# Pinned order, deeper prefetch and two moved constants on the GpSimd load queue of a linear-attention and spectral-mixing kernel

## The chip, the cores and the metric

One core of one Trainium2 chip. The metric is the device time of one execution in microseconds (us), the median of several runs; the trace is that of one of these runs. The program uses one core only, with the kernel before run beside each changed kernel on the same chip.

## The reference, cut to what matters

```python
# q, k, v: (8 batches, 8 heads, 576, 64) fp32
phi = lambda x: where(x > 0, x, exp(x) - 1) + 1
kv  = einsum('bhsd,bhse->bhde', phi(k), v);  z = sum(phi(k), axis=2)
x   = einsum('bhsd,bhde->bhse', phi(q), kv) / (einsum('bhsd,bhd->bhs', phi(q), z)[..., None] + 1e-6)
# x -> (8, 576, 512); 64 modes, each with complex weights of 512 x 512
X = rfft(x, axis=1)
Y[:, :64] = einsum('bmd,mde->bme', X[:, :64], w_r + 1j * w_i)
u = x + irfft(Y, n=576, axis=1)
out = u + maximum(u @ w_ch, 0)
```

The 128 weight matrices are most of the bytes. As bf16 on the chip each is 512 KB; one batch of q, of k or of v as fp16 is 576 KB.

## The kernel before

All large loads go through GpSimd's queue, because they change the type on the way (fp32 to fp16 or bf16). The attention stage makes the spectrum `xt_c`, batch by batch. Modes start only when the last batch's spectrum is there. Until then, weights can only be prefetched, into 8 buffers that stay and `W_PRE` buffers that are freed after the early modes. The framework's scheduler may reorder the instructions of an engine unless told otherwise.

```python
    nc.sync.dma_start(out=pick_sb, in_=pick_dr.ap())     # small constants, on SyncE's queue
    nc.sync.dma_start(out=inv_sb, in_=inv_dr.ap())
    # ... cut ...
    W_KEEP = 8
    def w_load(kk, half, pool, tag, bufs):
        name, src = (("wr", moe_w_r), ("wi", moe_w_i))[half]
        w = pool.tile([128, NDC, D], BF16, tag=tag, bufs=bufs, name=f"{name}{kk}")
        nc.gpsimd.dma_start(out=w, in_=src[kk].rearrange("(p dc) e -> p dc e", dc=NDC))
        return w
    W_PRE = 10
    # ... cut ...
    for b in range(B):                                    # attention, one batch at a time
        raw = {}
        for nm, src in (("q", q), ("k", k), ("v", v)):    # two buffers each
            t = sA.tile([128, NHP, NJ * Dh], F16, tag=f"{nm}16", bufs=2, name=f"{nm}16_{b}")
            nc.gpsimd.dma_start(out=t, in_=src[b].rearrange("h s d -> (h s) d").rearrange(
                "(hp r j) d -> r hp (j d)", r=128, j=NJ))
            raw[nm] = t
        if b >= 1:
            w_next()                                      # one prefetched weight per batch
        for nm in ("q", "k"):                             # ACT: exp; DVE: max, then min
            # ... cut ...
            for c in range(2):
                nc.vector.tensor_tensor(out=ev[:, c], in0=ev[:, c], in1=rv[:, c], op=ALU.min)
        nc.vector.tensor_copy(out=vp[:, :, :, 0:64], in_=raw["v"]...)   # the copy of v
        # ... cut: kv, numerators, spectrum of the batch into xt_c ...

    nc.gpsimd.dma_start(out=wch16, in_=moe_w_ch.rearrange("(c p) j -> p c j", p=128))
    while pending:
        w_next()                                          # the rest of the prefetch
    # ... cut: 64 modes, each with two weights; inverse transform ...
    def finish(t, by_act):                                # output stage
        # ... cut ...
        if by_act:
            nc.scalar.activation(out=r, in_=e, func=AF.Relu)
            nc.gpsimd.tensor_tensor(out=x, in0=x, in1=r, op=ALU.add)
```

The last use of the k buffer of batch b is the `min` of k, and DVE does it just after the copy of v of batch b+1 (its own order, shown below). The k load of batch b+2 needs that buffer. The constant `pick_sb` is an operand of a matmul in every mode, `inv_sb` one of the inverse transform.

Of the kernel before, what the change touches and what calls it, by code (L numbers as in the profile page):

```python
# [16 lines left out]
NJ = 9  # L17
# [36 lines left out]
def kernel(  # L54
# [10 lines left out]
    nc = tc.nc  # L65
# [5 lines left out]
    NDC = D // 128  # L71
# [9 lines left out]
    inv_dr = nc.inline_tensor(inv_np, name="dft_inv")  # L81
    pick_dr = nc.inline_tensor(pick_np, name="row_pick")
# [7 lines left out]
    inv_sb = const.tile([2 * NM, S], F16, name="inv_sb")  # L90
    pick_sb = const.tile([128, 16], F16, name="pick_sb")
    wch16 = const.tile([128, NDC, D], F16, name="wch16")
# [2 lines left out]
    nc.scalar.activation(out=actwarm, in_=actwarm, func=AF.Exp)  # L95
    nc.sync.dma_start(out=id16, in_=id16_dr.ap())
    nc.sync.dma_start(out=fwd_sb, in_=fwd_dr.ap())
    nc.sync.dma_start(out=pick_sb, in_=pick_dr.ap())
    nc.sync.dma_start(out=inv_sb, in_=inv_dr.ap())

    xt_c = xpool.tile([128, XTW], BF16, name="xt_c")
    nc.vector.memset(xt_c[:, NDC * XDC : XTW], 0.0)
# [15 lines left out]
    def w_load(kk: int, half: int, pool, tag: str, bufs: int):  # L118
        name, src = (("wr", moe_w_r), ("wi", moe_w_i))[half]
        w = pool.tile([128, NDC, D], BF16, tag=tag, bufs=bufs, name=f"{name}{kk}")  # L120
        nc.gpsimd.dma_start(out=w, in_=src[kk].rearrange("(p dc) e -> p dc e", dc=NDC))  # L121
        return w

    w_in: dict[int, list] = {}


    W_PRE = 10
    wpre_ctx, sA_ctx, psA_ctx = ExitStack(), ExitStack(), ExitStack()
    wpre = wpre_ctx.enter_context(tc.tile_pool(name="wpre", bufs=1))
    sA = sA_ctx.enter_context(tc.tile_pool(name="sA", bufs=1))  # L130
    psA = psA_ctx.enter_context(tc.tile_pool(name="psA", bufs=1, space=bass.MemoryType.PSUM))
    n_pre, n_keep = W_PRE // 2, W_KEEP // 2

# [6 lines left out]
    def w_next():  # L140
        kk, half = pending.pop(0)
        pool, tag, bufs = (wpool, "w", W_KEEP) if kk < n_keep else (wpre, "wp", W_PRE)
        w_in.setdefault(kk, []).append(w_load(kk, half, pool, tag, bufs))
# [17 lines left out]
    for b in range(B):  # L161
        raw = {}
        for nm, src in (("q", q), ("k", k), ("v", v)):
            t = sA.tile([128, NHP, NJ * Dh], F16, tag=f"{nm}16", bufs=2, name=f"{nm}16_{b}")
            nc.gpsimd.dma_start(
                out=t,
                in_=src[b].rearrange("h s d -> (h s) d").rearrange(
                    "(hp r j) d -> r hp (j d)", r=128, j=NJ
                ),
            )  # L170
            raw[nm] = t
        if b >= 1:
# [3 lines left out]
        for nm in ("q", "k"):  # L176

            e = sA.tile([128, 2, NJ, 2, Dh], F16, tag=f"{nm}e", bufs=2, name=f"{nm}e_{b}")
# [3 lines left out]
            for c in range(2):  # L182
                nc.scalar.activation(out=ev[:, c], in_=rv[:, c], func=AF.Exp)  # L183
            nc.vector.tensor_scalar(  # L184
                out=rf, in0=rf, scalar1=0.0, scalar2=1.0, op0=ALU.max, op1=ALU.add
# [6 lines left out]
            out=vp[:, :, :, 0:64], in_=raw["v"].rearrange("p a (j d) -> p a j d", d=Dh)  # L192
# [17 lines left out]
        for hpo in range(2):  # L210
            rows = slice(hpo * 64, hpo * 64 + 64)
            nc.scalar.copy(
                out=kv_sb[rows],
                in_=kv_ps[rows, :, 0:260].rearrange("p t (c o n) -> p c t o n", c=2, o=2)[
                    :, :, :, hpo, :
                ],
# [5 lines left out]
        for hpp in range(2):  # L222
            qT_ps = psA.tile([128, NJ, 2, NP], F16, tag="big", bufs=3, name=f"qTp{b}_{hpp}")
            for sl in range(NJ):
                j = 8 if sl == 8 else 4 * (sl % 2) + sl // 2
# [6 lines left out]
                out=qT[:, hpp].rearrange("p t (j r) -> p t j r", r=NP),  # L232
                in_=qT_ps.rearrange("p j t r -> p t j r"),
# [5 lines left out]
        for jj in range(NJJ + 1):  # L239
# [8 lines left out]
                out=dst.rearrange("p (o c d) -> p o c d", o=2, c=4),  # L248
# [19 lines left out]
    def w_get(kk: int):  # L268
        if kk not in w_in:
            w_in[kk] = [w_load(kk, half, wpool, "w", W_KEEP) for half in range(2)]  # L270
        return w_in.pop(kk)
# [24 lines left out]
                yt_ps[:, ec, kk % 8, :], st[:, ec * 128 : ec * 128 + 128], pick_sb  # L296
            )

    nc.gpsimd.dma_start(out=wch16, in_=moe_w_ch.rearrange("(c p) j -> p c j", p=128))
    while pending:  # L300
        w_next()
    psA_ctx.close()
    sA_ctx.close()
    psW = tc.alloc_tile_pool(name="psW", bufs=1, space=bass.MemoryType.PSUM)
# [170 lines left out]
    for b in range(B):  # L475
        ov = out[b].rearrange("(p j) d -> p j d", j=NJ)
        for jj in range(NJJ):
            finish(b * NJJ + jj, jj % 2 == 1)
            if jj % 2 == 1:
                for j2 in range(2):  # L480
                    (nc.sync, nc.scalar)[j2].dma_start(
                        out=ov[:, 4 * j2 + jj - 1 : 4 * j2 + jj + 1, :],
                        in_=x_main[b][j2 * 64 : j2 * 64 + 64, jj - 1 : jj + 1, :],
                    )
        if b % 2 == 1:
            i = b // 2
            finish(B * NJJ + i, False)
            for hf in range(2):
                (nc.sync, nc.scalar)[hf].dma_start(
                    out=out[2 * i + hf].rearrange("(p j) d -> p j d", j=NJ)[:, 8, :],  # L490
                    in_=x_tail[i][hf * 64 : hf * 64 + 64, :],
# [32 lines left out]
```

## Time and profile before

| Kernel before | |
|---|---|
| median time (range) | 454.02 us (453.87 to 454.76) |
| profiled span | 452.8 us |
| loads issued by GpSimd | 153, 81.80 MB landed |
| last spectrum copy | 123.84 us |
| matmul on the last weight | 400.38 us |

The page first. It names the engines PE (TensorE; PEld is its loading of operands), DVE (VectorE), ACT (ScalarE), POOL (GpSimd) and SP (SyncE); a q behind a name marks the engine's sequencer. The DMA row gives the busy share of the DMA engines in tenths, in 40 slices of the span (11.3 us each); the next row gives the bytes that landed per second in each slice. The last line is the chain of waits, by engine.

```profile
DMA  9999999999689999999999999999999999925884
GB/s 156 211 209 209 208 207 210 210 213 214 126 164 213 214 214 213 212 214 214 214 214 214 212 214 214 214 214 213 214 212 214 214 213 214 213 48 173 271 263 147
DMA 64%; PE 15%; DVE 11%; ACT 4%; issue 2%; POOL 1%; POOLq 0%; DVEq 0%; ACTq 0%; SPq 0%
```

The kernel is bound by its loads up to slice 35. 214 GB/s landed are 428 GB/s read, since the type is halved on the way. The Trainium skill ("DMA: Bandwidth & Descriptors", Bandwidth) has 425 GB/s for a 16 MB transfer on this path, so the queue runs at its rate here. The one gap is in slices 11 and 12 (126 and 164 GB/s). In stretches of 2 us, the view by windows shows it. Its columns are the stretch, its length, the busy time (and number of instructions) of PE, PEld, DVE, ACT and POOL, the granted clock, the DMA share and GB/s.

```profile
58.00:60.00 2.00, 0.72 (x13) 0.48 (x15) 2.00 (x8) 2.00 (x4) 1.09 (x2) 0.64 1.21 207
60.00:62.00 2.00, 1.81 (x24) 1.14 (x24) 2.00 (x6) 1.16 (x2) 0.94 (x2) 0.50 1.20 207
...
118.00:120.00 2.00, 1.31 (x12) 0.64 (x11) 1.93 (x7) 0.00 (x0) 0.00 (x0) 0.50 0.90 182
120.00:122.00 2.00, 1.53 (x10) 0.92 (x10) 0.41 (x1) 0.00 (x0) 0.00 (x0) 0.50 0.16 31
122.00:124.00 2.00, 1.08 (x7) 0.57 (x6) 0.69 (x1) 0.15 (x1) 0.00 (x0) 0.50 0.00 0
124.00:126.00 2.00, 1.72 (x16) 0.80 (x20) 0.49 (x1) 0.23 (x1) 0.53 (x1) 0.50 0.00 0
126.00:128.00 2.00, 2.00 (x21) 0.69 (x13) 0.26 (x2) 0.58 (x1) 1.59 (x3) 0.50 0.67 90
```

Missing bytes in the last five, against 214 GB/s: (32 + 183 + 214 + 214 + 124) x 2 / 214 = 7.2 us. That is the hole that the change aims at. At 58 to 62 us, inside attention, nothing is missing. GpSimd's timeline says why there is a hole (start, length, what was issued, and in brackets the idle time before it and what ended it):

```profile
46.36 0.74 POOL L165 DMA_DIRECT2D v_5_924<-in_v_dram  x1 [5.52 <-DVE rd_87 L245]
52.69 0.74 POOL L165 DMA_DIRECT2D q_5_920<-in_q_dram  x1 [5.58 <-issue]
...
58.91 0.74 POOL L165 DMA_DIRECT2D k_5_922<-in_k_dram  x1 [4.94 <-issue]
...
80.46 0.74 POOL L165 DMA_DIRECT2D k_7_1248<-in_k_dram  x1 [2.42 <-DVE ke_934 L188]
...
102.32 0.53 POOL L121 DMA_DIRECT2D wi_1430<-in_moe_w_i_dram  x1 [1.93 <-DMA wi_1414<-in_moe_w_i_dram]
125.27 0.53 POOL L121 DMA_DIRECT2D wr_1603<-in_moe_w_r_dram  x1 [22.42 <-PE P_1442 L279]
```

The last prefetched weight was issued at 102.32 us. The next load waited 22.42 us for mode 0's matmuls to free a buffer. The first lines show the scheduler's order: v_5 is issued 6.3 us ahead of q_5 and 12.6 us ahead of k_5, against the program's q, k, v. So v_5 had long landed when DVE came to it, and DVE went on to the min of k_4 without a wait:

```profile
66.94 0.75 DVE L191 COPY vpad_104<-v_5_924 128x2304 f16<-128x2304 f16 x1
67.61 1.42 DVE L188 TENSOR_TENSOR ke_771<-ke_771,k_4_759 128x1152 f16<-128x1152 f16 x2
```

On ACT, the last batch waited for q and for k, and its spectrum was done at 123.84 us:

```profile
94.33 2.22 ACT L183 ACTIVATE qe_1254<-q_7_1246 128x1152 f16<-128x1152 f16 x2 [3.25 <-DMA q_7_1246<-in_q_dram]
99.60 2.22 ACT L183 ACTIVATE ke_1260<-k_7_1248 128x1152 f16<-128x1152 f16 x2 [3.06 <-DMA k_7_1248<-in_k_dram]
...
123.84 0.38 ACT L265 ACTIVATE xt_c<-xf_1386 128x256 bf16<-128x256 f32 x1 [7.76 <-DVE xt_c L264]
```

First the matmul on the last weight in PE's timeline, then the last instructions of the program by line (count, then shortest, median and longest in ns, then the first and last start in us):

```profile
400.38 0.67 PE L285 MATMUL P_3689<-wi_3687,xt_c 128*32 128x512 bf16 x4 [1.82 <-DMA wi_3687<-in_moe_w_i_dram]
```

### The profile page before, as it was taken

To read this page: it belongs to the slowest core of one execution; us is meant where nothing else is said; L and a number is where in the kernel's file an instruction comes from. 1 tells how busy PE (TensorE), PEld (TensorE's weight loads), DVE (VectorE), ACT (ScalarE), POOL (GpSimd) and SP (SyncE) were. 2 spreads that over 40 slices of the span, in tenths; PEclk is the share of its full clock that TensorE was granted. 3 is DMA by queue.
4 is the path that set the end of the run, shared out by engine and by line. 5 is a ranking of instruction groups with operands and counts; after the bars stand their busy time and mean duration, and the time that the engine had idled before them with its cause. 6 is when DMAs were issued, how large, how long until landed. Compare 5 with 4: busy or idle time off the path is not lost.

```text
span 452.8 us, 6147 instructions
## 1 busy us (share of the span) xinstructions
PE 270.5 (60%) x2488; PEld 147.4 (33%) x2488; DVE 181.2 (40%) x329; ACT 136.8 (30%) x207; POOL 107.9 (24%) x173
## 2 busy tenths in 40 slices
PE   0353777767699777766777643233332399359870
PEld 0332555545434334333334321111110168113320
DVE  0672788865424353434344400100100022019990
ACT  3566256642224343343343411000000023013120
POOL 4222124210033222222212212122212221004650
PEclk9955556656556999999899975555555569559995
DMA  9999999999689999999999999999999999925884
GB/s 156 211 209 209 208 207 210 210 213 214 126 164 213 214 214 213 212 214 214 214 214 214 212 214 214 214 214 213 214 212 214 214 213 214 213 48 173 271 263 147
DMA packets 35691, 92.23 MB, mean 204 GB/s; under 512 B 3536, under 2 KB 16592, under 8 KB 35664
## 3 DMA queue, kind: packets, MB, share of 16 engines
q0 software_dynamic: 31632, 81.80, 93.1%
q1 hardware_dynamic: 2304, 5.20, 3.9%
q10 hardware_dynamic: 1728, 4.85, 3.4%
q8 instruction: 19, 0.31, 0.2%
q14 instruction: 8, 0.07, 0.0%
HBM read 163.93 MB, written 9.44 MB: 383 GB/s over the span
## 4 chain that ended last, share of the span: by engine, by line
DMA 64%; PE 15%; DVE 11%; ACT 4%; issue 2%; POOL 1%; POOLq 0%; DVEq 0%; ACTq 0%; SPq 0%
DMA wr_3038<-in_moe_w_r_dram 4%; DMA wi_2350<-in_moe_w_i_dram 4%; DMA k_7_1248<-in_k_dram 4%; DMA wi_2161<-in_moe_w_i_dram 4%; DMA wi_2009<-in_moe_w_i_dram 4%; DMA wr_2697<-in_moe_w_r_dram 4%; DMA wr_2861<-in_moe_w_r_dram 4%; DMA wr_3378<-in_moe_w_r_dram 4%; DMA wr_2546<-in_moe_w_r_dram 4%; DMA wr_3202<-in_moe_w_r_dram 4%; DMA wr_3480<-in_moe_w_r_dram 4%; DMA wi_1856<-in_moe_w_i_dram 4%; DMA wi_3687<-in_moe_w_i_dram 4%; DMA v_4_761<-in_v_dram 4%; DMA q_2_431<-in_q_dram 3%; DMA v_0_111<-in_v_dram 2%
## 5 line engine op out<-in xcount | busy, mean ns | idle before, releaser
L285 PEld LDWEIGHTS <-xt_c 128*32 128x32 bf16 x256 | 18.2, 156 | 70.5 <-issue 68.8
L279 PEld LDWEIGHTS <-xt_c 128*32 128x32 bf16 x256 | 15.4, 156 | 39.2 <-issue 21.8
L202 PE MATMUL kvp_126<-vpad_103,ke_119 64*128 64x130 f16 x36 | 2.1, 309 | 17.0 <-DVE ke_119 L188 17.0
L394 PEld LDWEIGHTS <-YT 128*112 128x112 f16 x32 | 7.7, 289 | 2.7 <-issue 2.2
L469 POOL TENSOR_TENSOR x_main_1583<-x_main_1583,r_3743 128x512 f32<-128x512 f32 x1 | 1.3, 1270 | 26.9 <-DVE x_main_1583 L465 26.9
L398 PEld LDWEIGHTS <-YT 128*112 128x112 f16 x32 | 7.5, 293 | 0.4
L202 PEld LDWEIGHTS <-ke_119 64*128 64x128 f16 x36 | 1.9, 141 | 17.0 <-DVE ke_119 L188 17.0
L152 PEld LDWEIGHTS <-qT_328 64*128 64x128 f16 (+1 forms) x80 | 2.6, 111 | 12.1 <-DVE x_1_351 L247 8.2
L121 POOL DMA_DIRECT2D wr_1603<-in_moe_w_r_dram x1 | 0.5, 531 | 22.4 <-PE P_1442 L279 22.4
L448 PEld LDWEIGHTS <-inv_sb 128*128 128x128 f16 x32 | 3.1, 97 | 7.3 <-issue 5.2
L444 PEld LDWEIGHTS <-id_64 128*128 128x128 f16 x32 | 3.1, 101 | 6.4 <-issue 2.4
L152 PE MATMUL num_3_386<-kv_79,qT_328 64*128 64x65 f16 x8 | 0.4, 239 | 7.9 <-DVE x_1_351 L247 7.9
L152 PEld LDWEIGHTS <-qT_165 64*128 64x128 f16 (+1 forms) x80 | 2.4, 120 | 7.5 <-ACT qT_165 L231 4.4
L291 DVE CAST ys_2962<-P_2953 128x512 f16<-128x512 f32 x1 | 0.7, 692 | 10.1 <-PE P_2953 L285 10.1
L184 DVE TENSOR_SCALAR q_0_107<-q_0_107 128x2304 f16<-128x2304 f16 x1 | 0.8, 760 | 9.7 <-ACT qe_113 L183 9.7
L152 PEld LDWEIGHTS <-qT_980 64*128 64x128 f16 (+1 forms) x80 | 2.5, 101 | 6.5 <-issue 3.4
L447 PEld LDWEIGHTS <-inv_sb 128*128 128x128 f16 x32 | 3.1, 97 | 4.4 <-issue 1.3
L291 DVE CAST ys_3679<-P_3670 128x512 f16<-128x512 f32 x1 | 0.7, 690 | 9.3 <-PE P_3670 L285 9.3
L291 DVE CAST ys_3391<-P_3382 128x512 f16<-128x512 f32 x1 | 0.7, 691 | 9.2 <-PE P_3382 L285 9.2
L291 DVE CAST ys_2809<-P_2800 128x512 f16<-128x512 f32 x1 | 0.7, 692 | 9.2 <-PE P_2800 L285 9.2
L291 DVE CAST ys_3051<-P_3042 128x512 f16<-128x512 f32 x1 | 0.7, 692 | 9.2 <-PE P_3042 L285 9.2
L291 DVE CAST ys_3429<-P_3420 128x512 f16<-128x512 f32 x1 | 0.7, 692 | 9.1 <-PE P_3420 L285 9.1
(1357 smaller groups left out, 857.6 us busy)
## 6 DMA issues: line engine op xcount, KB each, us to landing
q_0_107<-in_q_dram POOLq DMA_DIRECT2D x1, 576.0 KB, 7.8
k_0_109<-in_k_dram POOLq DMA_DIRECT2D x1, 576.0 KB, 9.7
v_0_111<-in_v_dram POOLq DMA_DIRECT2D x1, 576.0 KB, 11.8
q_1_268<-in_q_dram POOLq DMA_DIRECT2D x1, 576.0 KB, 13.9
k_1_270<-in_k_dram POOLq DMA_DIRECT2D x1, 576.0 KB, 16.0
v_1_272<-in_v_dram POOLq DMA_DIRECT2D x1, 576.0 KB, 18.1
q_2_431<-in_q_dram POOLq DMA_DIRECT2D x1, 576.0 KB, 14.5
k_2_433<-in_k_dram POOLq DMA_DIRECT2D x1, 576.0 KB, 13.3
```

Source lines behind the costliest of these rows:

```text
L152: nc.tensor.matmul(num[orow, hpo, c0 : c0 + 65], qT[rows, hpp, h2, cols], kv_sb[rows, hpp, h2, :])
L184: nc.vector.tensor_scalar(out=rf, in0=rf, scalar1=0.0, scalar2=1.0, op0=ALU.max, op1=ALU.add)
L202: nc.tensor.matmul(kv_ps[:, h2, hpp * 130 : hpp * 130 + 130], kp[rows, hpp, j].rearrange("p o d -> p (o d)"), vp[rows, hpp::2, j, 0:65], s ...
L279: nc.tensor.matmul(P[quad, :], xt_cols(dc, 1, kk), wr[:, dc, :], start=True, stop=False, tile_position=(0, dc * 32),)
L285: nc.tensor.matmul(P[quad, :], xt_cols(dc, 0, kk), wi[:, dc, :], start=False, stop=True, tile_position=(0, dc * 32),)
L291: nc.vector.tensor_copy(out=st, in_=P)
L394: nc.tensor.matmul(z_ps[: 2 * NE, :], lhs[ec], wch16[:, ec, :], start=(ec == 0), stop=(ec == NDC - 1))
L398: nc.tensor.transpose(y_ps[: 2 * NE, ec, :], lhs[ec], id16)
L444: nc.tensor.matmul(e, id16, e0_parts(t)[0][1], start=True, stop=False, skip_group_check=True)
L447: nc.tensor.matmul(y, lhs, YZ[b][:, 0, :])
L448: nc.tensor.matmul(e, lhs, YZ[b][:, 1, :], start=False, stop=True, skip_group_check=True)
L469: nc.gpsimd.tensor_tensor(out=x, in0=x, in1=r, op=ALU.add)
```

## The change

The intent: every load of the attention stage in program order, so that q and k of the last batches aren't overtaken; two more prefetched weights (ten modes) and two constants at the end of the prefetch, to fill the hole. The diff, with a wrapped load cut:

```diff
-    nc.sync.dma_start(out=pick_sb, in_=pick_dr.ap())
-    nc.sync.dma_start(out=inv_sb, in_=inv_dr.ap())
@@ w_load
-        nc.gpsimd.dma_start(out=w, in_=src[kk].rearrange("(p dc) e -> p dc e", dc=NDC))
+        tc.keep_in_program_order(
+            nc.gpsimd.dma_start(out=w, in_=src[kk].rearrange("(p dc) e -> p dc e", dc=NDC))
+        )
-    W_PRE = 10
+    W_PRE = 12
@@ loads of q, k and v
-            nc.gpsimd.dma_start( ... )
+            tc.keep_in_program_order(nc.gpsimd.dma_start( ... ))
@@ after attention
-    nc.gpsimd.dma_start(out=wch16, in_=moe_w_ch.rearrange("(c p) j -> p c j", p=128))
     while pending:
         w_next()
+    tc.keep_in_program_order(
+        nc.gpsimd.dma_start(out=wch16, in_=moe_w_ch.rearrange("(c p) j -> p c j", p=128))
+    )
+    tc.keep_in_program_order(nc.gpsimd.dma_start(out=pick_sb, in_=pick_dr.ap()))
+    tc.keep_in_program_order(nc.gpsimd.dma_start(out=inv_sb, in_=inv_dr.ap()))
```

More of the change, by code (lines that the diff above doesn't have):

```diff
@@ L164 @@
             t = sA.tile([128, NHP, NJ * Dh], F16, tag=f"{nm}16", bufs=2, name=f"{nm}16_{b}")
-            nc.gpsimd.dma_start(
-                out=t,
-                in_=src[b].rearrange("h s d -> (h s) d").rearrange(
-                    "(hp r j) d -> r hp (j d)", r=128, j=NJ
-                ),
+            tc.keep_in_program_order(
+                nc.gpsimd.dma_start(
+                    out=t,
+                    in_=src[b].rearrange("h s d -> (h s) d").rearrange(
+                        "(hp r j) d -> r hp (j d)", r=128, j=NJ
+                    ),
+                )
             )
@@ L297, in mode_product @@
             )
-    nc.gpsimd.dma_start(out=wch16, in_=moe_w_ch.rearrange("(c p) j -> p c j", p=128))
     while pending:
         w_next()
+    tc.keep_in_program_order(
+        nc.gpsimd.dma_start(out=wch16, in_=moe_w_ch.rearrange("(c p) j -> p c j", p=128))
+    )
+    tc.keep_in_program_order(nc.gpsimd.dma_start(out=pick_sb, in_=pick_dr.ap()))
+    tc.keep_in_program_order(nc.gpsimd.dma_start(out=inv_sb, in_=inv_dr.ap()))
     psA_ctx.close()
```

## The prediction

"Drain moves from 120.3" is the time at which the load queue runs empty.

> **What bounds the kernel now.** The page shows the DMA engines at 90% or more in nearly every slice up to 390 us: 214 GB/s in the mode stage, 206 to 212 while q, k and v stream. The chain of waits is 64% DMA; from 145 us it is one weight load after another until the last lands at 400.4 us. 52 us follow without loads (inverse transform, output), which the change leaves alone. So time = loaded bytes / rate + idle time of the load queue + 52 us, and only the idle time can be won.
>
> The DMA rates of stretches of 2 us show one large hole: 182, 31, 0, 0, 90 GB/s from 118 to 128 us, against 214 GB/s about 7.2 us. GpSimd's timeline says why: the last prefetched weight was issued at 102.3 us, and the next issue (125.3 us) needs mode 0's products to free a buffer. Mode 0 starts at 124.3 us, after the last batch's spectrum is copied.
>
> **What the change does.**
> 1. Two more prefetched weights, 512 KB each, 2.45 us each at 214 GB/s: 4.9 us more work before the hole.
> 2. pick and inv (148 KB, about 0.7 us) go from the start to the end of the prefetch: another 0.7 us in the hole.
> 3. Program order: the comparison of instruction orders shows that in the attention stage only GpSimd's order changes. Before, other loads went ahead of q_7 and k_7; k_7 landed at 99.6 us and ACT stood 3.1 us for it (3.3 us for q_7), with copies of older batches behind it. In program order k_7 should land near 87 us, v_7 near 90 us. So attention should end about 2 us sooner, near 122 us.
>
> **Cost side.** v_5 to v_7 can't overtake q and k any more. DVE needs v of batch b+1 before it finishes k of batch b, which frees the buffer for k of batch b+2. That loop: copy 0.7 + minimum 1.4 + issue 0.5 + 1.9 until data flows (wr_1603, issued at 125.3 us into an empty queue, shows bytes from about 127.1) + k and v 2.8 each + landing 0.5 = 10.6 us, against 3 x 2.83 + 2.45 = 10.9 us of DMA and about 11.0 us of computing per batch. The queue stays just fed; I allow 0 to 2 us of bubbles, an estimate. The Trainium skill ("DMA: Bandwidth & Descriptors", the anatomy of a SWDGE DMA) gives about 2.0 us of fixed cost per DMA; here wr_1603 took 5.0 us less 2.45 of data, 2.5 us.
>
> pick now lands last, near 127 us, so mode 0's gather matmul waits and PE stalls 2 to 4 us after about 2.5 modes. Their buffers are free by then (five loads, 12 us of queue), so this should not reach the queue. One more early mode (1.3 us of PE) is covered: the queue had 10 us of slack at 136 us.
>
> **Sum.** Drain moves from 120.3 to about 126 us, new loads are issued from about 123 us: the hole closes. 454.0 - 7.2 + 0.7 (bubbles) = 447.5 us, 1.4% faster. Range 445.8 to 450.5. Faster by over 2% would need 9 us, more than the idle there is. Chances: 0.05 faster, 0.94 within 2%, 0.01 slower.
>
> **What would show it.** No slice between 105 and 140 us below 200 GB/s; last weight landing near 393 us; 52 us behind it; ACT's waits for q_7 and k_7 gone; last spectrum copy near 122 us; a PE wait for pick.
>
> **What would make it wrong.** Head-of-line bubbles in attention (below 200 GB/s at 60 to 95 us); attention ending after 124 us; the pick wait holding back the releases of modes 2 and on; a changed rate of mixed loads.

## More of the kernel before

```profile
L519 POOLq DRAIN  x3: 45/102/11355, 440.4 to 452.5; - x3
L519 SPq DRAIN  x3: 7/7/7, 448.4 to 452.0; - x3
```

At its end GpSimd has a `DRAIN`, an instruction that the kernel's code does not ask for (the profile puts it to the framework's line `with TileContext`), of 11.36 us, from 440.38 to 451.73 us in the trace. Its last add ends at 442.41 us, so 9.3 us of the `DRAIN` lie behind all of GpSimd's work that the program asks for. SyncE has confirmed the last stores at 448.47 us. The program ends only after both, so it stands 451.73 - 448.47 = 3.26 us for GpSimd alone.

## The result

| | before | after |
|---|---|---|
| median time (range) | 454.02 us (453.87 to 454.76) | 450.03 us (448.93 to 450.39) |
| ratio to before | | 0.9905, 95% interval 0.9885 to 0.9925 |
| last spectrum copy | 123.84 us | 127.15 us |
| matmul on the last weight | 400.38 us | 399.83 us |
| stores confirmed (SyncE) | 448.47 us | 447.46 us |
| GpSimd's DRAIN | 440.38 to 451.73 us | 439.77 to 442.80 us |
| profiled span | 452.8 us | 448.5 us |

A ratio is the mean time of one kernel's fast runs over that of the other's of the same rounds, so not quite the ratio of the medians. By the time alone the prediction holds: 450.03 us lies inside 445.8 to 450.5, near its edge. By the trace the last weight, which should have come 7 us earlier, came 0.55 us earlier. The profile after, the same views:

```profile
DMA  8999999999999999999999999999999999953897
GB/s 139 209 210 209 208 177 179 178 214 213 214 192 216 212 215 213 214 213 214 213 214 214 213 214 213 214 213 213 214 213 214 213 214 213 214 104 92 275 284 217
```

Slices 11 and 12 have 214 and 192 GB/s now. But slices 6 to 8 fell from about 209 to about 178 GB/s, and the first slice from 156 to 139. By windows:

```profile
58.00:60.00 2.00, 0.34 (x9) 0.25 (x9) 2.00 (x6) 2.00 (x3) 0.70 (x1) 0.50 1.07 184
60.00:62.00 2.00, 1.81 (x25) 1.10 (x21) 2.00 (x7) 1.54 (x2) 1.32 (x3) 0.50 0.70 77
62.00:64.00 2.00, 2.00 (x29) 1.66 (x28) 2.00 (x4) 0.00 (x0) 0.00 (x0) 0.50 1.16 196
...
72.00:74.00 2.00, 1.26 (x19) 0.77 (x19) 2.00 (x6) 1.28 (x2) 1.81 (x3) 0.50 0.73 94
74.00:76.00 2.00, 2.00 (x29) 1.57 (x31) 1.91 (x4) 0.00 (x0) 0.21 (x1) 0.50 0.99 157
...
84.00:86.00 2.00, 0.84 (x17) 0.60 (x17) 2.00 (x8) 2.00 (x3) 1.20 (x2) 0.50 0.91 154
86.00:88.00 2.00, 1.81 (x26) 1.13 (x22) 2.00 (x5) 0.76 (x1) 2.00 (x4) 0.50 0.84 92
...
130.00:132.00 2.00, 0.39 (x1) 0.10 (x1) 0.00 (x0) 0.23 (x1) 2.00 (x5) 0.50 0.74 110
```

The first seven lines lack (23 + 130 + 11 + 113 + 50 + 53 + 115) x 2 / 207 = 4.8 us of loading: three new bubbles, one per batch. The last line is what is left of the hole, (214 - 110) x 2 / 214 = 1.0 us. GpSimd's timeline and DVE's copies of v show what the bubbles wait for:

```profile
59.30 0.74 POOL L166 DMA_DIRECT2D k_5_920<-in_k_dram  x1 [5.49 <-issue]
...
72.19 0.74 POOL L166 DMA_DIRECT2D k_6_1083<-in_k_dram  x1 [6.61 <-ACT qe_926 L185]
72.92 0.75 POOL L166 DMA_DIRECT2D v_6_1085<-in_v_dram  x1
...
84.80 0.74 POOL L166 DMA_DIRECT2D k_7_1246<-in_k_dram  x1 [5.77 <-ACT qe_1089 L185]
...
129.63 0.54 POOL L120 DMA_DIRECT2D wr_1622<-in_moe_w_r_dram  x1 [11.63 <-PE P_1461 L287]
```

```profile
69.56 0.76 DVE L193 COPY vpad_102<-v_5_922 128x2304 f16<-128x2304 f16 x1 [2.45 <-PE num_2_699 L152]
70.23 1.42 DVE L190 TENSOR_TENSOR ke_769<-ke_769,k_4_757 128x1152 f16<-128x1152 f16 x2
...
82.17 0.76 DVE L193 COPY vpad_101<-v_6_1085 128x2304 f16<-128x2304 f16 x1 [1.81 <-DMA v_6_1085<-in_v_dram]
```

This is a closed loop. v_5 lands at 69.4 us (the page's list of issues: 9.4 us after its issue at 60.03). DVE copies it at 69.56 us and then ends the min of k_4 at 71.65 us. That frees the buffer, and k_6 is issued at 72.19 us. v_6 stands behind k_6 in program order and lands at 82.1 us (9.2 us after 72.92). DVE copies it at 82.17 us, and so on. One turn takes 12.6 us. (In before, v_5 had been issued at 46.36 us, landed at 62.1 and was copied at 66.94 without a wait.) The label "ACT qe_926" in the bracket of k_6 is only what ended last by the profile's reckoning before that issue; the buffer is freed by DVE. In the same way the copy of v_5 names PE, though v_5 had landed only about 0.1 us before.

The attention stage therefore ends later, the pick constant makes PE wait 1.88 us, and the last weight comes 0.55 us earlier:

```profile
127.15 0.38 ACT L267 ACTIVATE xt_c<-xf_1384 128x256 bf16<-128x256 f32 x1 [7.75 <-DVE xt_c L266]
```

```profile
132.27 0.25 PE L297 MATMUL yt_1445<-pick_sb,ys_1455 128*128 128x16 f16 x4 [1.88 <-DMA pick_sb<-row_pick]
...
399.83 0.67 PE L287 MATMUL P_3689<-wi_3687,xt_c 128*32 128x512 bf16 x4 [1.77 <-DMA wi_3687<-in_moe_w_i_dram]
```

```profile
L525 POOLq DRAIN  x3: 46/102/3027, 439.8 to 448.0; - x3
L525 SPq DRAIN  x3: 7/7/7, 447.4 to 447.7; - x3
```

GpSimd's DRAIN takes 3.03 us in place of 11.36, ends 1.0 us after its last add and before the stores do. The span's 4.3 us are: 0.55 from the last weight, 0.46 between it and the confirmed stores, and 3.26 because nobody waits for GpSimd any more.

How closely do two traces agree? d2 below is after with two idle instructions more, and its last weight is used at 398.24 us, 1.6 us earlier than in after. The timed runs of after alone span 448.93 to 450.39 us, and its trace is of the slowest of them. So a difference of less than about 1.6 us between single traces of the pinned kernels is not resolved. The unpinned ones agree better: 400.38 to 400.58 us in before, d1, f2 and f3.

So there are two questions. Where did 7 us of filled hole go? And what makes the DRAIN short?

### The profile page after: what moved, and what is told of

Its sections match the earlier page's. It is cut to its first block, busy times and chain, and to the rows that moved or that the text cites. A ratio compares the mean times of both kernels' runs of the same rounds, so it can differ in the third digit from the quotient of the medians.

```text
span 448.5 us, 6143 instructions
## 1 busy us (share of the span) xinstructions
PE 272.3 (61%) x2488; PEld 150.6 (34%) x2488; DVE 180.7 (40%) x329; ACT 136.8 (31%) x207; POOL 109.7 (24%) x175
## 4 chain that ended last, share of the span: by engine, by line
DMA 70%; PE 10%; DVE 8%; issue 4%; ACT 3%; POOL 2%; POOLq 0%; ACTq 0%; DVEq 0%; SPq 0%
DMA wr_3038<-in_moe_w_r_dram 4%; DMA wi_1423<-in_moe_w_i_dram 4%; DMA wr_3378<-in_moe_w_r_dram 4%; DMA wr_2367<-in_moe_w_r_dram 4%; DMA wi_1820<-in_moe_w_i_dram 4%; DMA wr_2205<-in_moe_w_r_dram 4%; DMA wr_2697<-in_moe_w_r_dram 4%; DMA wr_2861<-in_moe_w_r_dram 4%; DMA wr_2520<-in_moe_w_r_dram 4%; DMA wr_3202<-in_moe_w_r_dram 4%; DMA wi_3687<-in_moe_w_i_dram 4%; DMA wr_3480<-in_moe_w_r_dram 4%; DMA wr_2026<-in_moe_w_r_dram 4%; DMA v_4_759<-in_v_dram 4%; DMA q_2_429<-in_q_dram 3%
## 5 line engine op out<-in xcount | busy, mean ns | idle before, releaser
L152 PEld LDWEIGHTS <-qT_326 64*128 64x128 f16 (+1 forms) x80 | 2.8, 115 | 13.5 <-DVE x_1_349 L249 8.8
L152 PEld LDWEIGHTS <-qT_163 64*128 64x128 f16 (+1 forms) x80 | 2.7, 112 | 8.2 <-ACT qT_163 L233 4.4
L152 PEld LDWEIGHTS <-qT_652 64*128 64x128 f16 (+1 forms) x80 | 2.5, 107 | 8.7 <-DVE x_3_675 L249 3.3
L152 PEld LDWEIGHTS <-qT_978 64*128 64x128 f16 (+1 forms) x80 | 2.5, 112 | 6.4 <-DVE x_5_1001 L249 2.7
## 6 DMA issues: line engine op xcount, KB each, us to landing
v_0_109<-in_v_dram POOLq DMA_DIRECT2D x1, 576.0 KB, 11.4
```

The lines of the kernel that those rows point to most:

```text
L152: nc.tensor.matmul(num[orow, hpo, c0 : c0 + 65], qT[rows, hpp, h2, cols], kv_sb[rows, hpp, h2, :])
```

## The experiments

"Weight" is the start of the matmul on the last weight, "stores" is SyncE's confirmation, "DRAIN" is the long one of GpSimd; the figures of before and after are repeated.

| kernel | median us | ratio to before (95%) | weight | DRAIN us | stores | span |
|---|---|---|---|---|---|---|
| before | 454.02 | | 400.38 | 11.36 | 448.47 | 452.8 |
| after | 450.03 | 0.9905 (0.9885 to 0.9925) | 399.83 | 3.03 | 447.46 | 448.5 |
| e1_pre12 | 449.22 | 0.9886 (0.9869 to 0.9903) | 395.08 | 11.35 | 442.60 | 447.4 |
| e2_pin_pre12 | 449.41 | 0.9889 (0.9871 to 0.9907) | 399.22 | 2.86 | 447.42 | 448.2 |
| e3_pin | 453.12 | 0.9970 (0.9957 to 0.9984) | 402.25 | 2.86 | 449.58 | 450.7 |
| e4_consts | 450.15 | 0.9910 (0.9895 to 0.9925) | 399.86 | 2.86 | 447.96 | 449.1 |
| e5_pin_k3 | 448.73 | 0.9878 (0.9863 to 0.9892) | 398.63 | 2.86 | 446.34 | 447.1 |
| e6_pre12_consts | 446.35 | 0.9827 (0.9811 to 0.9844) | 395.95 | 2.86 | 443.65 | 444.7 |
| d1_before_pad4 | 454.20 | 1.0001 (0.9986 to 1.0016) | 400.58 | 11.36 | 448.64 | 452.7 |
| d2_after_pad2 | 449.40 | 0.9895 (0.9879 to 0.9911) | 398.24 | 3.03 | 445.73 | 446.9 |
| f1_vfirst | 444.44 | 0.9779 (0.9764 to 0.9794) | 393.68 | 3.03 | 441.48 | 442.7 |
| f2_wch_rows (wrong) | 454.14 | 0.9992 (0.9973 to 1.0012) | 400.54 | 11.19 | 448.03 | 452.7 |
| f3_early_end | 450.91 | 0.9924 (0.9909 to 0.9939) | 400.42 | 11.37 | 447.45 | 448.7 |
| g1_qkv_rows (wrong) | 448.24 | 0.9862 (0.9846 to 0.9879) | 398.01 | 6.13 | 445.74 | 446.8 |

The texts name rival theories by letters or short names. What was weighed against what is said in plain words under each.

### e1_pre12: the deeper prefetch alone

On the kernel before:

```diff
-    W_PRE = 10
+    W_PRE = 12
```

> Kernel before with twelve prefetched weights instead of ten, nothing else. Stream theory: the 7.2 us hole of the load queue shrinks by 4.9 us, the last weight lands near 395 us instead of 400.4. Drain theory A (the 11.4 us GpSimd drain at the end of the program goes with the 153 loads on the GpSimd queue, 155 make it short): drain still about 11 us, time about 448.5 to 449.5. Rival B (the drain is short because of the prefetch depth): drain about 3 us, time about 445.5. Rival C (the drain goes with program order): as A here.

Measured: 449.22 us. The last weight is used at 395.08 us, 5.3 us earlier, against 4.9 us that two weights are worth at the queue's rate. Nothing else moved; the DRAIN is long as before. So this line alone wins as much time as the whole change, and by the way that was intended.

### e2_pin_pre12: the change without the moved constants

On the kernel after, the two constants back on SyncE's queue at the start:

```diff
+    nc.sync.dma_start(out=pick_sb, in_=pick_dr.ap())
+    nc.sync.dma_start(out=inv_sb, in_=inv_dr.ap())
-    tc.keep_in_program_order(nc.gpsimd.dma_start(out=pick_sb, in_=pick_dr.ap()))
-    tc.keep_in_program_order(nc.gpsimd.dma_start(out=inv_sb, in_=inv_dr.ap()))
```

> The changed kernel with the two constants back on the Sync queue at the start (program order and twelve weights kept, 153 GpSimd loads). Theory A: last weight lands near 399.5 us as in the changed kernel, drain about 11 us again, time about 453 us, and the PE wait for pick is gone without gain. Rivals B and C: drain stays about 3 us, time about 450 us.

Measured: 449.41 us, the same as after. The weight is used 0.6 us earlier than after (399.22), which is less than after and d2 differ by, so a cost of the move is not shown by this pair. The first slice shows where one can arise. It has 153 to 159 GB/s in the eight kernels that load the constants on SyncE at the start (g1 left out), and 139 to 152 in the five that do not: on the mean 8 GB/s less, about 0.4 us of loading by my estimate from these rates. The Trainium skill ("DMA: Bandwidth & Descriptors", Issuing engines are not separate DMA queues) says that loads from all issuing engines share the same 16 DMA engines. The traces fit: in the first slice GpSimd's queue does not yet fill these engines (the later ones of attention have about 209 GB/s), and there the loads on SyncE raise the rate. The DRAIN is short (2.86 us) with 153 loads on GpSimd's queue, as many as before. The two extra loads are not needed to make it short.

### e3_pin: program order alone

As e2, and `W_PRE = 10`.

> Program order alone (ten weights, constants on Sync). Stream theory: about 5 us of bubbles in the attention stage at 60, 73 and 86 us as in the changed kernel, and a hole of 4 to 5 us at about 126 to 130 us remains, so the last weight lands 2 to 3 us later than before, near 403 us. Theory A and B: long drain, time about 456.5 us. Rival C: short drain, about 453 us.

Measured: 453.12 us, 0.3% faster. The last weight comes 1.9 us later than before (402.25): pinning the order costs load time. It shows bubbles at the places where after has them, and the hole is still there:

```profile
58.00:60.00 2.00, 0.69 (x13) 0.45 (x15) 2.00 (x8) 2.00 (x3) 1.06 (x2) 0.50 0.96 164
60.00:62.00 2.00, 1.81 (x24) 1.14 (x26) 2.00 (x6) 1.19 (x2) 0.96 (x2) 0.50 0.78 96
...
72.00:74.00 2.00, 1.82 (x27) 1.20 (x28) 1.97 (x6) 1.34 (x2) 1.60 (x3) 0.50 0.66 65
```

It is faster all the same, because the DRAIN is short: the program ends 1.1 us after the stores, and 4.3 us after them in before.

### e4_consts: the moved constants alone

On the kernel before, unpinned:

```diff
-    nc.sync.dma_start(out=pick_sb, in_=pick_dr.ap())
-    nc.sync.dma_start(out=inv_sb, in_=inv_dr.ap())
@@ after the prefetch
     while pending:
         w_next()
+    nc.gpsimd.dma_start(out=pick_sb, in_=pick_dr.ap())
+    nc.gpsimd.dma_start(out=inv_sb, in_=inv_dr.ap())
```

> Kernel before with only the two constants moved to the end of the prefetch on the GpSimd queue (155 GpSimd loads, no program order, ten weights). Stream theory: last weight lands 0 to 0.7 us sooner than before. Theory A: drain about 3 us, so time about 450.5 us. Rivals B and C: drain about 11 us, time about 453.5 us.

Measured: 450.15 us, as fast as after, with a last weight only 0.5 us earlier than before. The DRAIN is short again. So either part, the pin or the two loads, makes the DRAIN short by itself, and the theory that it is the pinned order alone falls too.

### d1_before_pad4 and d2_after_pad2: is it the count of GpSimd's instructions?

The long DRAIN might have come from where GpSimd's instruction stream happened to end. Four dummy instructions on the kernel before, two on the kernel after:

```diff
+    gpad = const.tile([128, 4], F32, name="gpad")          # [128, 2] in d2
+    for i in range(4):                                      # range(2) in d2
+        nc.gpsimd.memset(gpad[:, i : i + 1], 0.0)
```

> Kernel before with four one-column memsets on GpSimd ahead of the first load, which nothing reads: GpSimd's stream grows from 329 to 333 instructions, nothing else changes. Alignment theory (the 11.4 us drain appears only when the end of GpSimd's instruction stream falls in a narrow place: seen at 327 and 329 instructions, not at 324, 326, 326 and 331): drain about 3 us, time about 451.2 us, last weight still near 400 us. Rival (the drain follows the order or set of the loads): drain about 11.4 us, time about 454.4 us.

> The changed kernel with two such memsets: GpSimd's stream grows from 326 to 328 instructions. Alignment theory: drain about 11.4 us, time about 453.3 us. Rival (order or set of the loads): drain stays about 3 us, time about 450 us.

Measured: no effect. 454.20 us and a DRAIN of 11.36 us with four more on before; 449.40 us and 3.03 us with two more on after. The theory of the instruction count falls, at least for these two offsets.

### e5_pin_k3: program order with a third k buffer

If the bubbles come from the loop over k's buffer, a third buffer must remove them, with the order still pinned. On e3:

```diff
-            t = sA.tile([128, NHP, NJ * Dh], F16, tag=f"{nm}16", bufs=2, name=f"{nm}16_{b}")
+            t = sA.tile([128, NHP, NJ * Dh], F16, tag=f"{nm}16", bufs=(3 if nm == "k" else 2), name=f"{nm}16_{b}")
```

> Program order alone (ten weights, constants on Sync), with three buffers for k instead of two, so that k of batch b+2 need not wait for DVE to finish k of batch b. Bubble theory (the dips at 60, 73 and 86 us are the head of the GpSimd queue waiting for k's buffer): the dips shrink to less than half, load queue idle there falls from about 4.5 us to under 2 us, unless q's buffer becomes the next head wait. Rival (dips come from the rate of the loads themselves or from v): dips stay. Profile of program order alone to compare: last software load 401.9 us. Stream: 323 instructions, short drain by the alignment theory.

Measured: 448.73 us, 4.4 us faster than e3, and the bubbles are gone:

```profile
58.00:60.00 2.00, 0.85 (x17) 0.61 (x17) 2.00 (x8) 2.00 (x3) 0.00 (x0) 0.74 1.20 205
60.00:62.00 2.00, 1.82 (x28) 1.14 (x22) 2.00 (x5) 0.93 (x1) 0.00 (x0) 0.50 1.22 209
...
72.00:74.00 2.00, 1.90 (x27) 1.47 (x29) 1.91 (x5) 1.18 (x2) 0.00 (x0) 0.50 1.21 207
```

The last weight comes 3.6 us earlier than in e3 and the last spectrum copy at 122.04 us. The cause of the bubbles is settled: it is the buffer of k, not the pin as such. Three k buffers together with twelve prefetch buffers did not fit in the on-chip memory (the build failed), so that pair was not run.

### e6_pre12_consts: the change without the pin

e4 with `W_PRE = 12`.

> Twelve weights and the constants at the end of the prefetch, without program order. Stream theory: last software load near 394.5 us, no dips in the attention stage, 5 us sooner than with program order. Alignment theory (329 instructions): long drain of 11.4 us, time about 449 us. Rival (constants on GpSimd make the drain short, as they did alone): drain 3 us, time about 445.7 us.

Measured: 446.35 us, 3.7 us faster than after, with the scheduler's own order. The last weight is used at 395.95 us, 3.9 us earlier than in after. That is the price of the pinned order, measured as the only difference between e6 and after apart from the place of one other load (`wch16`). Against d2, the quicker twin of after, it is 3.05 us in time. The short DRAIN stays, where a count that decides by alignment had been expected to make it long. Against e1 the last weight comes 0.9 us later, and the traces put most of that in the hole: 2.6 us are missing there in e6, 1.6 us in e1. The first load after the prefetch is issued 2.47 us after the last spectrum copy in e6 (125.82 us) and 1.43 us after it in e1 (124.73 us): it waits for mode 1's second weight in e6, and for mode 0's first in e1. The same 2.5 us stand in after, d2 and f1, which also have twelve weights and the moved constants, and the same 1.4 us in before, e2 and e4. Why the release moves is not shown.

### f1_vfirst: pinned order, v loaded first

The loop goes through v: v of batch b+1 stands behind k of batch b+1 in the pinned order. If v comes first, it does not wait for k's buffer, and the loop is cut without a buffer more. The scheduler's own order in before had done this: v_5 ahead of q_5 and k_5. On the kernel after:

```diff
-        for nm, src in (("q", q), ("k", k), ("v", v)):
+        for nm, src in (("q", q), ("k", k), ("v", v)) if b == 0 else (("v", v), ("q", q), ("k", k)):
```

> The changed kernel with one reordering: from batch 1 on, v is loaded ahead of q and k, so that DVE's copy of v of batch b+1, which stands ahead of the last operation on k of batch b, no longer waits behind q and k of b+1. If the bubbles are the loop v -> DVE -> k's buffer -> head of the queue: the dips at 60, 73 and 86 us go, attention ends near 122 us, the hole at 130 us goes with it (twelve weights last until about 126 us), the last software load ends near 394 us and the time is about 443 to 444 us with a short drain. If k's buffer holds the head whatever v does: dips stay, time about 449 us.

Measured: 444.44 us, ratio 0.9779: the only kernel here that is over 2% faster, and the best of all. It has no bubble and no hole:

```profile
GB/s 146 208 208 208 211 208 209 208 214 214 213 219 214 213 214 213 214 214 213 213 213 214 214 212 213 214 214 213 213 213 214 214 214 214 213 77 113 275 277 214
```

The last spectrum copy is at 116.02 us, 11.1 us earlier than in after, and the last weight is used at 393.68 us, which is what the prediction had expected of the change. PE stands 7.6 us for the pick constant in this kernel, since modes start earlier; the load queue does not notice (every slice after the eighth is at 212 or above up to the last weights).

### f3_early_end: is the DRAIN fixed work that starts when GpSimd is done?

On the kernel before, GpSimd's last two adds, those of batch 7, given to DVE:

```diff
-            finish(b * NJJ + jj, jj % 2 == 1)
+            finish(b * NJJ + jj, jj % 2 == 1 and b < B - 1)
```

> Kernel before with the last two GpSimd additions (batch 7) given to DVE, so that GpSimd has nothing to do from about 438.6 us on instead of 442.4. Theory G (the long drain is a piece of work of fixed length, about 9.3 us after GpSimd's last operation, that only starts when GpSimd comes to its end): drain ends near 448 us, below or at the end of the stores, time about 451 us in spite of about 1 us more on DVE. Rival H (the drain waits for something outside GpSimd that ends near 451.7 us): the program still ends at about 452.8 us in the profile or later, time about 454 us.

Measured: 450.91 us with an unchanged load stream (last weight 400.42 us).

```profile
L519 POOLq DRAIN  x3: 45/93/11370, 436.6 to 448.4; - x3
L519 SPq DRAIN  x3: 7/7/7, 447.4 to 448.2; - x3
```

The last add now ends at 438.60 us in place of 442.41, and the DRAIN ends at 447.92 us: 9.3 us behind it, exactly as in before (451.73 - 442.41). It is work of a given length that begins when GpSimd has done its adds, and not a wait for something else at the end of the program, which would have ended when it did before. It also shows that its end was on the critical path: in both kernels it ends last, and the span fell by 4.1 us (the median of the timed runs by 3.3, against before in the same rounds) with the stream untouched.

### f2_wch_rows and g1_qkv_rows: does the DRAIN grow with the pieces that the loads were cut into?

Both load the right bytes into wrong places: the result is wrong (relative errors 0.65 and 1.26), the work is the same. A load of longer consecutive rows is cut into fewer pieces. On the kernel before, f2 and g1:

```diff
-    nc.gpsimd.dma_start(out=wch16, in_=moe_w_ch.rearrange("(c p) j -> p c j", p=128))
+    nc.gpsimd.dma_start(out=wch16, in_=moe_w_ch.rearrange("(p c) j -> p c j", p=128))
```

```diff
-                    "(hp r j) d -> r hp (j d)", r=128, j=NJ
+                    "(r hp j) d -> r hp (j d)", r=128, j=NJ
```

> Wrong result on purpose: kernel before with the channel weights loaded in the row order that the mode weights have (the same bytes to the same tile, fewer and longer pieces), everything else the same, order and waits of GpSimd too. Theory D (the long drain depends on how many pieces the loads put on the software queue, in which sequence): the sequence shifts by 24 pieces per DMA engine, drain most likely short (3 us), time about 451 us. Rival E (it depends on the order of the loads, their count or their waits): drain stays 11.4 us, time about 454 us.

> Wrong result on purpose: kernel before with all 24 loads of q, k and v in whole rows (9 KB per partition in one stretch instead of four), the same bytes, order, count and waits, but some 24 x 24 = 576 fewer pieces per DMA engine in the software queue. Theory D2 (the drain grows with the piece count's place in a ring that begins again at some place, the kernel before lying just below it: 24 fewer pieces took 0.17 us off the drain in the run with the channel weights in rows): 576 fewer pieces take about 4 us off, a drain clearly between 3 and 11 us, about 7 us, and the end of the program no longer waits for it (time about 451 us or less, the loads may also run at 214 instead of 209 GB/s). Rival E (order, count or waits of the loads decide): drain stays 11.2 to 11.4 us. Rival F (two states only, decided by the pieces): drain 3 us.

Measured, f2: 31,248 packets on GpSimd's queue in place of 31,632, 24 fewer on each of the 16 engines; DRAIN 11.19 us, 0.17 less, and no change of time. It did not become short. g1: 22,416 packets, 576 fewer on each engine.

```profile
L519 POOLq DRAIN  x3: 45/102/6130, 438.2 to 446.5; - x3
L519 SPq DRAIN  x3: 7/7/7, 445.7 to 446.0; - x3
```

The DRAIN is 6.13 us, 5.2 us less: 5.2 / 576 = 9 ns for each piece on each engine, and f2's 0.17 / 24 = 7 ns is of the same size. So within the order of the kernel before, the long DRAIN grows with the number of pieces that went through GpSimd's queue. The Trainium skill ("DMA: Bandwidth & Descriptors", SWDGE vs HWDGE vs iDMA) says that on this path a core of GpSimd computes the descriptors in software and writes them into rings in on-chip memory. That would make GpSimd the place for work per piece; no run here shows what the work is. g1 was 1.4% faster than before, partly by the stream too (weight 2.4 us earlier).

## Why the prediction was right in time and wrong in its reasons

- **"the hole closes"**: right. 7.2 us became 1.0 us, and e1 shows the two weights worth 5.3 us.
- **"pick now lands last ... this should not reach the queue"**: right. The wait was 1.88 us, just under the 2 to 4 us forecast, and in f1 even 7.6 us did not reach the queue.
- **The moved constants**: placed in the hole as a gain of 0.7 us in filling, with no loss counted. With twelve weights no gain is seen: the last weight comes 0.6 us later with them (after against e2, not resolved) and 0.9 us later (e6 against e1). What is seen is a first slice slower by about 0.4 us, and a first load after the prefetch that is released 1.0 us later. With ten weights (e4) the move gained 0.5 us.
- **"The queue stays just fed; I allow 0 to 2 us of bubbles"**: wrong, and the main error. The loop was seen, but its sum of 10.6 us was too small; it took 12.6 us. Copy and min were right (2.1 us predicted, 69.56 to 71.65 us measured), and so was the issue (0.5 and 0.54 us). The term that was mis-sized is from the issue of k to the landing of v: 1.9 + 2.8 + 2.8 + 0.5 = 8.0 us predicted, and 9.9 us measured for batch 6 (72.19 to 82.1 us), 10.1 us for batch 5 (59.30 to 69.4). The allowance around a load, 1.9 us ahead of it and 0.5 us behind, came from one weight that was issued into an empty queue. 12.6 us against 10.9 us of loads per batch starves the queue by about 1.7 us per batch; three bubbles show it, 4.8 us in all.
- **"attention should end about 2 us sooner, near 122 us"**: wrong for the same reason: 127.15 us. The waits of ACT for q_7 and k_7 did go (94.87 and 96.99 us, without a wait), but a batch now takes the loop's time. e5 (122.04) and f1 (116.02) show what the order does when the loop is cut.
- **"52 us follow without loads ... which the change leaves alone"**: wrong. From the last weight to the span's end it was 52.4 us before and is 48.7 us after, of which 3.26 us is GpSimd's DRAIN leaving the end. I had read this stage as a sum and had not looked at what ends last in it.

Put together, for these two traces: the hole gave 6.2 us, the bubbles took 4.8, the slower start (156 to 139 GB/s in the first slice) about 0.9, and so the last weight should come about 0.5 us earlier; 0.55 was measured, which is closer than two traces repeat. The end of the program gave 3.7 us. The prediction's sum was -7.2 + 0.7 us on the stream and nothing behind it. So the stream fell short by about 6 us, and the end gave 3.7 us that nobody had counted. These errors of opposite sign cancelled in part, and that the time still fell inside the range was luck.

Open: what makes the DRAIN short. It is 11.2 to 11.4 us in before, e1, d1, f2 and f3, and 2.9 to 3.0 us in every kernel that pins the order, or that puts the two constants at the end of the queue, or both. The number of loads, the pin alone, the number of GpSimd's instructions and a count of pieces by itself are each refuted as the sole reason: e3 has the same 31,632 packets as before. One idea left is that the work depends on where in its ring the queue stands at the end; nothing here tests it. The 0.46 us between the last weight and the stores was not followed up either; it is no more than before (48.09 us) and f2 (47.49 us) differ there, with the same output stage.

## What to carry to other kernels

Before pinning a queue's order, write down each loop of the form "load waits for buffer, buffer waits for a consumer, consumer waits for a load behind the first one", and take issue-to-landing times from the busy stretch itself; if the loop is near the period, break it by order (load first what frees the other's buffer, as with v here) or by one buffer. Test the parts of a bundled change alone: one line of this one gave as much as the whole, another cost 4 us of loading. And look at what ends last in the program, down to the closing instructions: here 3 us at the end depended on nothing that the change meant to touch.

## What the Trainium skill lacked or had wrong

- "VectorE: DVE Perf Modes", section The DRAIN you can't avoid: it calls the DRAINs of a program's start and end about 12 ns, constant, on all five engines. If the closing DRAINs of these kernels, which the profile puts to the line `with TileContext`, are of that kind, this does not hold. On SyncE they took 7 ns here; GpSimd's longest took 11,355 ns in one kernel and 3,027 ns in the other, and the former was on the critical path for 3.26 us.
- No page that I read gives that cost or says what it depends on. "DMA: Bandwidth & Descriptors" (SWDGE vs HWDGE vs iDMA) would be the place: 5.2 us less for 576 fewer pieces on each DMA engine, about 9 ns each (g1), and a jump from 11.4 to 2.9 us for the same number of packets in another order (e3), which is unexplained.
- "DMA: Bandwidth & Descriptors", section Anatomy of one DMA: SWDGE path, gives about 2.0 us of fixed cost per load. One weight issued into an empty queue took 5.0 us, less 2.45 of data, so 2.5 us. What the section does not say is how these costs add up for loads queued one behind another. In the pinned loop, k and v together took 9.9 to 10.3 us from k's issue to v's landing, less 2 x 2.8 of data, so 4.3 to 4.7 us, nearer to two fixed costs than to one. What part of it is the rest of the load ahead (q_6's bytes still came until 74.7 us, 2.5 us after k_6's issue) the runs don't separate.
